# Nine opening products of zeros, 512 columns wide, become 36 of 128 columns

## The chip, the cores and the metric

The kernel runs on one core of a Trainium2 chip. The metric is the device time of one execution in microseconds, from several runs of which the median is given. Engines are named as in the profile: PE is TensorE's matmul row, PEld its weight loads, DVE is VectorE, ACT is ScalarE, POOL is GpSimd, SP is SyncE, which here issues most of the DMAs.

## The reference

For x of 2048 rows and 512 columns, the output mixes two branches with a gate per row. Branch a is a filter in the two-dimensional Fourier domain, branch b is a two-layer network with 1792 hidden features.

```python
g = sigmoid((x * gate_w).sum(-1, keepdims=True))
X = rfft2(x) * (w_r + 1j * w_i)          # 2048 x 257
a = irfft2(X, s=(2048, 512))
h = gelu(x @ w1 + b1)                    # 2048 x 1792
b = h @ w2 + b2
return g * a + (1 - g) * b
```

The opening products that this case is about compute nothing of this: both operands are zeros and the result is never read.

## The kernel before, in words

The 2048 rows are cut into 16 tiles of 128. A forward pass per tile folds x into even and odd parts on VectorE (`eo`, then `w`, L593 and L596), multiplies them by a cosine and sine table `cf` on PE (results `pd`), and transforms along the rows with a table `tf` (results `py`). Twiddles, the filter, and the inverse (`pz`, `pa`) follow later. The network's first layer is done for two of its fourteen feature blocks as plain products (results `ph`), for the others by a seven-product scheme (`nu`, `ux`); the second layer gives `po`, in the last group `dm`, `dn`, `dx`, `dz` and `dl`.

Most products are in the type float32r, which holds fewer bits than float32; a float32 operand is then split into a high and a low part and takes three products. Some, among them `pd` and the first `ph` products from the raw tile `war`, take plain float32 operands. All matmuls go through the helper `mm`, so the profile gives them one line, L420; the tile names tell them apart. A plain float32 matmul stands in the profile as two pairs of weight load and product, a float32r one as one pair.

Every piece of work is a step that is added to a graph with its engine, an estimated cost, what it reads and what it writes. The order in which the steps are emitted is a list of step numbers written out in the source (`ORDER`), and the buffers' places are another (`SLOTS`). The costs in the `add` calls are not used when the order is replayed. Each engine runs its own instructions in that order.

At the start, VectorE sets a 128 by 128 tile `zero` to 0 (L501). As soon as it is there, the step `warm` issues nine matmuls of `zero` by `zero` into a PSUM bank named `none` (`WARM = 9`). The moving operand is `zero` read four times over by an access pattern that repeats it, so that each has 512 columns. Three filler steps of 256 columns (`FILL = 3`) are in the order too: one directly behind the nine, one after the first four records of `ph`, one among the first `pd` records. On PE the order at the start is thus: nine opening products, a filler, four records of `ph`, a filler, twelve of `ph`, six of `pd`, a filler, more of `pd`.

Meanwhile the first x tile (`xf`, in two halves), two halves of the raw first-layer weights (`war`), the table `cf` and the gate weights (`g`) arrive by DMA. VectorE copies four sums of the gate weights into spare columns of `cf` (L547); the first `pd` product reads `cf` and waits for that copy. Behind it, ACT and DVE split `pd` into a high and a low part (`zb`), and PE takes those for `py`.

Of the kernel before, what the change touches and what calls it, by code (L numbers as in the profile page):

```python
# [354 lines left out]
def tile_kernel(ctx: ExitStack, tc: tile.TileContext, xt, xc, w1, w2, b1, b2, x0g, wf, wrev, out, consts):  # L355
# [18 lines left out]
    def buf(tag, shape, dt=F32, name="", parts=1, pool=None, cls=None, full=False, onto=False):  # L374
        slots.setdefault(tag, 1)
        return Buf(g, pool or (pp if tag in PSUM else sb if tag in whole else sc), tag, shape, dt, name, parts, cls, full, onto)

    def bank(shape, name, cls, full=False, onto=False, parts=1):
        return buf("ps", shape, F32, name, parts, None, cls, full, onto)
# [39 lines left out]
    def mm(ps, w, x, start, stop, **more):  # L419
        pe.matmul(ps, w, x, start=start, stop=stop, **more)  # L420
# [4 lines left out]
    def bcast(ap, *ns):  # L425
        return bass.AP(tensor=ap.tensor, offset=ap.offset, ap=[list(ap.ap[0]), *[[0, n] for n in ns], list(ap.ap[1])])
# [72 lines left out]
    FILL, WARM, NBARE = 3, 9, 1  # L499
    zero, none = buf("w", [P, P], F32R, "zero", cls="zero"), bank([P, 4, P], "none", "none", full=True)  # L500
# [3 lines left out]
    act_first.table = "gelu"  # L504

    def warm():
        for _ in range(WARM):
            mm(none.ap(), zero.ap(), bcast(zero.ap(), 4), True, True)

    add("pe", 0.09 + 0.427 * WARM, 0.1, warm, [zero], [none])  # L510

    for _ in range(FILL):
# [870 lines left out]
```

## Time and profile before

| | before |
|---|---|
| median of 3 runs | 354.13 us (353.65 to 354.32) |
| profiled execution, its own time | 353.74 us |
| its span, first to last instruction | 352.0 us |
| PE busy | 344.8 us, 1742 matmul records |
| PEld busy | 291.9 us, 1742 weight loads |
| DVE busy | 333.4 us |
| ACT busy | 301.6 us |
| opening products (128x512) | 9 records, 1.07 us to about 5.1 us |
| fillers (128x256) | 3 records, at 5.07, 5.60 and 8.55 us |
| first `pd` record | 7.86 us |

Busy times are unions of the records of an engine. Times in views of the profile are microseconds from the first instruction, unless a column says ns. PE works on products in a pipeline, so a record's length holds the way through the array as well as the columns; the distance from one start to the next tells what a product costs. A record may be shown to start while its engine still waits for the load or the product ahead. A view line of the form "start, length, engine, line, operation, out<-in, shapes, xcount" merges neighbours of one kind, and its length is then from the first start to the last end.

### The profile page before, as it was taken

Reading aid. Unit: us, or ns where it says so; the run is one execution under the profiler, and the core shown is the slowest. Engines: PE = TensorE matmul, PEld = TensorE weight load, DVE = VectorE, ACT = ScalarE, POOL = GpSimd, SP = SyncE. Lnnn points to the kernel's source line nnn. Section 1 sums busy time; section 2 is a strip of 40 time slices with the busy share of each in tenths; the row PEclk is TensorE's granted clock in tenths of the full one; section 3 lists DMA queues with packets and bytes.
Section 4 is the critical chain, followed back from the end, with each engine's and each line's share of the span. In section 5 each row is a group of like instructions: output and inputs, shape, how many; then the busy total and the mean of one; then the engine's idle time right before and its main releaser. Section 6 shows DMA issues by size and latency. Waiting matters only on the chain.

```text
span 352.0 us, 5796 instructions
## 1 busy us (share of the span) xinstructions
PE 344.8 (98%) x1742; PEld 291.9 (83%) x1742; DVE 333.4 (95%) x700; ACT 301.6 (86%) x631; POOL 56.6 (16%) x75
## 2 busy tenths in 40 slices
PE   8999999999999999999999999999999999999993
PEld 7988888888878888888888888888888889888883
DVE  5999999899999999999999999999999999999991
ACT  4999999999999665999759885599999999999622
POOL 2012002000003100121301301000120001463420
PEclk9999999999999999999999999999999999999998
DMA  7998896847879949999999845965582547898995
GB/s 227 378 283 287 242 300 179 226 110 288 212 239 240 183 164 294 298 225 266 240 245 239 174 116 119 298 228 180 173 175 66 148 135 208 156 152 189 196 205 198
DMA packets 47719, 74.63 MB, mean 212 GB/s; under 512 B 5544, under 2 KB 18344, under 8 KB 47688
## 3 DMA queue, kind: packets, MB, share of 16 engines
q1 hardware_dynamic: 37528, 58.42, 50.6%
q0 software_dynamic: 9728, 15.51, 27.3%
q10 hardware_dynamic: 432, 0.33, 0.3%
q8 instruction: 14, 0.23, 0.3%
q14 instruction: 17, 0.14, 0.1%
HBM read 52.02 MB, written 17.31 MB: 197 GB/s over the span
## 4 chain that ended last, share of the span: by engine, by line
PE 96%; DVE 1%; DMA 1%; issue 0%; ACT 0%; DVEq 0%
PE po L420 37%; PE uxB L420 11%; PE uxA L420 9%; PE nuB L420 8%; PE nuA L420 7%; PE pd L420 4%; PE pz L420 4%; PE py L420 3%; PE pa L420 3%; PE ph L420 3%; PE dx L420 3%; DMA xf<-in_x0g 1%; PE dm L420 1%; PE dn L420 1%; PE dz L420 1%; DVE eo L593 0%
## 5 line engine op out<-in xcount | busy, mean ns | idle before, releaser
L429 ACT ACTIVATE s<-po 128x512 f32<-128x512 f32 x40 | 23.1, 597 | 3.3 <-PE po L420 3.2
L968 ACT ACTIVATE po<-s 128x512 f32<-128x512 f32 x40 | 23.7, 598 | 0.3
L836 ACT ACTIVATE sw<-y,keep 64x512 f32<-64x512 f32 x32 | 22.5, 719 | 0.6
L775 DVE TENSOR_TENSOR m<-y,wf 128x514 f32<-128x514 f32 x32 | 21.3, 690 | 0.2
L420 PE MATMUL py<-zb,tf 128*128 128x258 f32 x96 | 20.2, 291 | 0.0
L420 PE MATMUL pd<-cf,w 128*128 128x129 f32 x128 | 18.5, 276 | 0.5 <-DVE cf L547 0.5
L420 PEld LDWEIGHTS pd<-cf,w 128*128 128x128 f32 x128 | 16.8, 191 | 1.8 <-DVE cf L547 0.7
L420 PE MATMUL pz<-tg,pq 128*128 128x128 f32 x128 | 18.3, 274 | 0.0
L420 PEld LDWEIGHTS py<-zb,tf 128*128 128x128 f32 x96 | 16.1, 189 | 2.5
L420 PEld LDWEIGHTS pz<-tg,pq 128*128 128x128 f32 x128 | 17.3, 190 | 1.0
L420 PE MATMUL nuB<-xB,wB0h 128*128 128x512 f32 x56 | 17.5, 393 | 0.0
L420 PE MATMUL pa<-zb,ci 128*128 128x256 f32 x96 | 17.0, 287 | 0.0
L420 PEld LDWEIGHTS pa<-zb,ci 128*128 128x128 f32 x96 | 15.1, 188 | 2.0
L978 ACT ACTIVATE s<-po,b2t 128x512 f32<-128x512 f32 x16 | 11.0, 693 | 6.8 <-PE po L420 6.6
L420 PE MATMUL nuA<-xA,wA0h 128*128 128x512 f32 x48 | 15.0, 393 | 0.0
L632 DVE TENSOR_TENSOR zb<-pd,zb 128x256 fp32r<-128x256 f32 x32 | 13.3, 420 | 0.8 <-ACT logit L631 0.8
L652 ACT ACTIVATE y<-pys 64x257 f32<-64x257 f32 x32 | 13.3, 417 | 0.6
L596 DVE TENSOR_TENSOR w<-eo 128x256 f32<-128x256 f32 x32 | 13.1, 419 | 0.1
L593 DVE TENSOR_TENSOR eo<-xf 128x256 f32<-128x256 f32 x32 | 12.7, 419 | 0.0
L840 DVE TENSOR_TENSOR pq<-y,sw 128x256 f32<-128x256 f32 x32 | 12.5, 416 | 0.2 <-ACT sw L836 0.2
L628 ACT ACTIVATE zb<-pd 128x256 fp32r<-128x256 f32 x32 | 12.1, 392 | 0.4 <-PE pd L420 0.4
L420 PEld LDWEIGHTS nuB<-xB,wB0h 128*128 128x128 f32 x56 | 10.4, 188 | 2.0
(595 smaller groups left out, 1262.6 us busy)
## 6 DMA issues: line engine op xcount, KB each, us to landing
wf<-in_wf SPq DMA_DIRECT2D x16, 257.0 KB
xf<-in_xt SPq DMA_DIRECT2D x14, 256.0 KB, 5.0
tf<-tf SPq DMA_DIRECT2D x16, 192.0 KB, 6.1
wrA<-in_w SPq DMA_DIRECT2D x12, 256.0 KB, 4.9
xbA<-in_xc SPq DMA_DIRECT2D x8, 256.0 KB, 5.7
xbB<-in_xc SPq DMA_DIRECT2D x8, 256.0 KB, 3.4
bacc<-s SPq DMA_DIRECT2D x8, 256.0 KB, 6.3
w<-bacc POOLq DMA_DIRECT2D x8, 256.0 KB, 4.4
```

The lines of the kernel that those rows point to most:

```text
L420: pe.matmul(ps, w, x, start=start, stop=stop, **more)
L429: a(lambda: act.activation(o.ap(), i.ap(), AF.Copy, scale=scale), n, [i], [o])
L593: v(lambda s=s, op=op: vec.tensor_tensor(eo.ap()[:, s], x.ap()[:, 0:2], x.ap()[:, 2:4], op=op), 256, [x], [(eo, s)])
L596: v(lambda s=s, op=op: vec.tensor_tensor(w.ap()[:, s], eo.ap()[:, :, 0], eo.ap()[:, :, 1], op=op), 256, [eo], [(w, s)])
L628: a(lambda c=c: act.activation(segs(xh, c), both(c), AF.Copy), 256, [ps[c]], [(xh, c)])
L632: v(lambda c=c: vec.tensor_tensor(segs(xl, c), both(c), segs(xh, c), op=ALU.subtract), 256, [ps[c], (xh, c)], [(xl, c)])
L652: a(lambda o=o, i=i: act.activation(Y[j].ap()[o:o + HP, 1], pys.ap()[i:i + HP, 1], AF.Copy), 257, [(pys, 1)], [(Y[j], 1 + k)], more=0.07)
L775: v(lambda mk=mk, k=k, y=y, w=w: vec.tensor_tensor(mk.ap(), y.ap(), w.ap()[:, k:k + 1, :ND].to_broadcast([P, 2, ND]), op=ALU.mult), 514, [ ...
L836: a(lambda sw=sw, y=y, o=o, i=i: act.activation(sw.ap()[o:o + HP], y.ap()[i:i + HP], AF.Copy, scale=keep.ap()[i:i + HP]), 512, [y, keep, * ...
L840: v(lambda sw=sw, pq_=pq_, y=y, k=k, op=op: vec.tensor_tensor(pq_.ap()[:, k], y.ap()[:, k], sw.ap()[:, 1 - k], op=op), 256, [y, TURNED[c], ...
L968: a(lambda ps=ps, n=n, o=o: act.activation(ps.ap(), o.ap()[:, n], AF.Copy), size, [o], [ps], more=0.04)
L978: a(lambda o=o, ps=ps, q=q: act.activation(o.ap(), ps.ap(), AF.Identity, bias=b2t.ap()[:, q:q + 1]), 600, [b2t, ps], [o])
```

## The change

The step `warm` issues 36 matmuls in place of nine. Each has the same 128 by 128 zeros as weights, and the same zeros, read once, as the moving operand, so 128 columns. They write the four quarters of the bank `none` in turn. The number of columns is the same in all, 9 x 512 = 36 x 128. The step keeps its place in the order, and the three fillers stay as they are.

```diff
     def warm():
-        for _ in range(WARM):
-            mm(none.ap(), zero.ap(), bcast(zero.ap(), 4), True, True)
+        for n in range(4 * WARM):
+            mm(none.ap()[:, n % 4], zero.ap(), zero.ap(), True, True)
 
     add("pe", 0.09 + 0.427 * WARM, 0.1, warm, [zero], [none])
```

## The prediction

> **What bounds the kernel now.** I read the page's head and its chain of waits first, to know which engine a lost microsecond must be lost on.
>
> ```profile
> span 352.0 us, 5796 instructions
> PE 344.8 (98%) x1742; PEld 291.9 (83%) x1742; DVE 333.4 (95%) x700; ACT 301.6 (86%) x631; POOL 56.6 (16%) x75
> PEclk9999999999999999999999999999999999999998
> PE 96%; DVE 1%; DMA 1%; issue 0%; ACT 0%; DVEq 0%
> ```
>
> TensorE (PE) is 96% of the chain that ended last. What is not PE lies at the two ends, so next comes the chain in order of time over the first 20 us.
>
> ```profile
> 0.75 3.18 DMA xf<-in_x0g
> ...
> 7.72 0.09 DVE cf L547
> 7.81 0.04 issue
> 7.86 0.94 PE pd L420 x6
> 8.79 0.12 PE none L420
> 8.91 1.11 PE pd L420 x10
> ```
>
> The opening products do not stand in it. The end is set by the first x tile landing (0.75 to 3.93), VectorE's work on it up to the copy into cf, and from 7.86 us on by PE. So PE has slack before 7.86 us. After it, I ask for the busy time of the long middle and for everything that PE's matmul and weight-load rows waited for.
>
> ```profile
> 8.00:346.00 338.00, 337.98 (x1714) 286.35 (x1715) 329.26 (x684) 297.37 (x622) 54.82 (x63) 1.00 0.79 213
> PE none L420 <- DVE zero L501: 1.1, 1, 1.1
> PE pd L420 <- DVE cf L547: 0.5, 1, 0.5
> PEld none L420 <- DVE zero L501: 1.1, 1, 1.1
> PEld pd L420 <- DVE cf L547: 0.7, 1, 0.7
> PEld pd L420 <- ACT y L648: 0.4, 2, 0.2
> PEld uxA L420 <- ACT uxA L429: 0.4, 1, 0.4
> PEld nuA L420 <- ACT gate L1292: 0.4, 1, 0.4
> PEld pown L420 <- DMA wf<-in_wf: 0.4, 1, 0.4
> PEld dx L420 <- DVE dz L1064: 0.2, 1, 0.2
> ```
>
> In the first line the matmul busy time is the first number after the width: 337.98 of 338.00 us. The second and third say that the matmuls waited twice in all, for the zeros and for cf. A delay that PE carries past 7.86 us meets almost nothing that could absorb it. The later weight-load waits are 1.8 us together; all but one are on ACT or DVE results that come from PE's own products and move with it. The one on a DMA (0.4 us) might give back up to 0.4.
>
> **The opening, product by product.** The timeline, asked in windows so narrow that each instruction stands alone (start, length, engine, what), printed to 0.01 us:
>
> ```profile
> 1.07 0.29 PEld L420 LDWEIGHTS none<-zero 128*128 128x128 f32 x1 [1.07 <-DVE zero L501]
> 1.23 0.34 PEld L420 LDWEIGHTS none<-zero 128*128 128x128 f32 x1
> 1.66 0.33 PEld L420 LDWEIGHTS none<-zero 128*128 128x128 f32 x1
> ...
> 1.66 0.63 PE L420 MATMUL none<-zero 128*128 128x512 f32 x1
> 4.65 0.63 PE L420 MATMUL none<-zero 128*128 128x512 f32 x1
> 5.07 0.33 PE L420 MATMUL none<-zero 128*128 128x256 f32 x1
> 5.24 0.27 PE L420 MATMUL ph<-xf,war 128*128 128x128 f32 x1
> 7.06 0.28 PE L420 MATMUL ph<-xf,war 128*128 128x128 f32 x1
> 7.86 0.38 PE L420 MATMUL pd<-cf,w 128*128 128x129 f32 x1 [0.52 <-DVE cf L547]
> ...
> 5.08 0.23 PEld L420 LDWEIGHTS ph<-xf,war 128*128 128x128 f32 x1
> 5.24 0.19 PEld L420 LDWEIGHTS ph<-xf,war 128*128 128x128 f32 x1
> ...
> 5.73 0.19 PEld L420 LDWEIGHTS ph<-xf,war 128*128 128x128 f32 x1
> 5.84 0.19 PEld L420 LDWEIGHTS ph<-xf,war 128*128 128x128 f32 x1
> ...
> 7.86 0.19 PEld L420 LDWEIGHTS pd<-cf,w 128*128 128x128 f32 x1 [0.71 <-DVE cf L547]
> 7.96 0.19 PEld L420 LDWEIGHTS pd<-cf,w 128*128 128x128 f32 x1
> ...
> 344.95 1.09 PE dl L420 x9
> 15.29 2.74 PE ph L420 x12
> 5.80 1.54 PE L420 MATMUL ph<-xf,war 128*128 128x128 f32 x12
> ```
>
> Four readings.
>
> First, order. Each product has a weight load of its own, even though the weights are the same zeros, and a load starts when the product before it starts: load at 1.66 with product at 1.66, load at 5.08 with product at 5.07, load at 5.24 with product at 5.24. It starts no earlier. So loads and products run one step apart, and the step is the longer of two things: the product's columns, or the load.
>
> Second, the clock. Products of 512 columns start at 1.66 and 4.65, seven steps of (4.65 - 1.66)/7 = 0.427 us. The same width later takes 2.74/12 = 0.228. The opening runs at half speed, although the page's clock row shows full speed throughout. A load is 0.33 us long in the opening and 0.19 after 5.24; the one at 5.08 is 0.23, between them. I put the change of speed at 5.15 us, 3.92 us after the first product got going at 1.23 (its load started at 1.07; the second load, which goes with the first product's start, at 1.23).
>
> Third, the load at full speed. Where PE had been waiting, a load is not covered by a product, and the step from it to the next load is the bare time from load to product: 7.96 - 7.86 = 0.10 and 5.84 - 5.73 = 0.11. I take 0.11. Products of 256 columns (dl, 1.09/9 = 0.12) and the fp32 pieces of ph (1.54 us for 12, of which the last takes 0.28: 1.26/11 = 0.115) just cover it. No product in this kernel is short enough to uncover it in a row; the change makes 36 that are.
>
> Fourth, the load at half speed. The bare first one is 1.23 - 1.07 = 0.16, but that record is 0.29 long where its neighbours are 0.33 and 0.34, so it may have begun 0.04 or 0.05 before its record, which gives 0.21. Twice the full-speed 0.10 to 0.11 gives 0.20 to 0.22. I take 0.21 and keep 0.16 as the lower end.
>
> **The change part by part.** It removes nine products of 512 columns and adds 36 of 128. Columns: 9 x 512 = 36 x 128, nothing there. Weight loads: 9 become 36, the 27 new ones are the cost. Outputs, semaphores and the other engines' work are untouched; 54 more PE instructions at the start are costed at nothing, covered by the 0.11 to 0.21 us that each pair occupies.
>
> - Width alone, at half speed: 0.427/4 = 0.107 a product, less than the load's 0.21. So the load sets the step.
> - Before 5.15 us: (5.15 - 1.23)/0.21 = 18.7 products. The other 17.3 at 0.11 take 1.91. The block ends, and the filler of 256 columns behind it starts, at 7.06 instead of 5.07: 1.99 us late.
> - That filler then runs at full speed: 0.12 instead of 5.24 - 5.07 = 0.17, which gives 0.05 back.
> - PE's cover: the last ph product starts at 7.06 and its columns are through some 0.11 later, at 7.17; the first pd product gets going at 7.96 with the second load. 7.96 - 7.17 = 0.79 us is free. With PE late, cf is there long before it is wanted, and the wait on it goes; nothing else is late next, since the DVE chain to cf uses no PE result.
> - Sum: 1.99 - 0.05 - 0.79 = +1.15 us at the first pd product, and past it all of it reaches the end.
>
> The profiled execution took 353.74 us (span 352.0 and 1.74 around it), 0.39 below the median of 354.13. Against itself the sum is 354.89; against the median it is 355.28. I forecast **355.3**.
>
> Bounds of the one unknown, the step: with 0.16 and half of it, 24.5 products are done by 5.15 and 11.5 x 0.08 = 0.92 follow, end 6.07, late 1.00, net +0.16 after the 0.05 and the 0.79 (0.84 together). With 0.22 and, at full speed, the 0.12 of dl, 17.8 and 18.2 x 0.12 = 2.18, end 7.33, late 2.26, net +1.42. I take the value near the upper end because the bare full-speed loads, 0.10 and 0.11, have no shortened record to explain away. A change of speed that comes 0.5 us earlier or later than 5.15 moves the changed kernel by 0.25 and leaves the kernel before alone, because the 0.79 covers it there.
>
> [...]
>
> **The rivals.**
>
> - *The loads are covered* (the other side: not slower). If a load took no longer than 0.107 at half speed, the 36 products would need 36 x 0.107 = 3.84 us, the block would end at 5.07 as before, and the time stays 354.1. For it: at 512 columns the half-speed steps show no trace of the load. Against it: the bare 0.16 at 1.07, and every load starting only with the product before. It decides at a step of 0.15, where the lateness just fills the 0.79.
> - *A shorter load*: step 0.16 then 0.08, net +0.2 to +0.3, 354.4, within what can be told from no change. [...] Against it: the two bare full-speed loads.
> - *The clock stays low longer.* The array's columns are then in use only half of the time (0.107 of 0.21), and if the speed depends on use, the change at 5.15 may come late. One more stretch of 3.92 us would put it at 9.07. All 36 then run at 0.21, end 8.79; the stretch from filler to the end of ph (7.17 - 5.07 = 2.10, less the 0.05), with 0.14 lost to the last 0.28 us of low speed, end at 10.98 against 7.96: +3.0, 357.1. For it: only that use halves. Against: the array is never idle for long. [...]
> - *Narrow products of this type run as slowly as plain fp32.* One fp32 product of 128 columns is two of ph's pieces, 2 x 0.11 = 0.22 at full speed, 0.43 at half. Then 9.2 are done by 5.15, 26.8 x 0.22 = 5.90 follow, end 11.05, net 5.98 - 0.84 = +5.14, 359.3. For it: no product of the one-pass type below 256 columns exists here. Against: at 256 columns (0.12 a product) it is still one pass, and nothing in the rows points to a step below.
> - *Faster*: PE cannot gain before 7.86 us because cf is not there earlier; only chance in the later order could do it.
>
> **How the numbers follow.** My forecast, +0.7 to +1.4 with PE's later waits passing it on: 0.54. Shorter load, +0.1 to +0.7: 0.15. Covered: 0.10. Clock late: 0.09. Slow type: 0.09. Faster: 0.03. About 0.2% (0.7 us) is what a measurement of this kernel can tell from no change. Same is covered and shorter load, plus 0.04 of the forecast for a partial give-back of the 0.4: 0.29. Slower is 0.50 + 0.09 + 0.09 = 0.68. The range goes from the covered case less the scatter of the runs, 353.9, to the late clock, 357.2; it leaves out the slow type and faster, 0.12.
>
> **What would show it.** In the profile after, the rows of none<-zero are 36 products of 128 columns; right if they start 0.21 apart, then 0.11, and the 256-column filler starts near 7.1 us. The wait of pd on cf disappears from PE's waits, the first pd product gets going near 9.1 us, and the span is about 353.2. A step of 0.107 shows the loads covered; 0.16 and 0.08 the shorter load; 0.21 throughout, and 0.33-long loads beyond 5.3 us, the late clock; 0.43 the slow type. The forecast also fails if pd is 1 us late but the end is not: then a wait further down took the delay in, and the weight-load waits listed above would have shrunk.

## The result and the profile after

The changed kernel takes 357.75 us (median of 6 runs, 356.28 to 358.81) against 354.02 (6 runs of the kernel before, 353.53 to 355.13). The ratio is 1.0109, with a 95% interval of 1.0090 to 1.0129: 3.73 us slower. The forecast was 355.3 with a range to 357.2, so the direction was right and the size and the range were wrong. The profiled execution took 356.28 us, the lowest of the six.

The page of the changed kernel, then its chain of waits in order of time (start, length, what):

```profile
span 354.5 us, 5850 instructions
PE 349.3 (99%) x1769; PEld 297.6 (84%) x1769; DVE 333.7 (94%) x700; ACT 301.5 (85%) x631; POOL 56.5 (16%) x75
PE 98%; ACT 0%; issue 0%; DVE 0%
```

```profile
1.07 8.26 PE none L420 x37
9.33 0.85 PE ph L420 x4
10.18 0.21 PE none L420
10.39 1.82 PE ph L420 x12
12.21 0.67 PE pd L420 x6
```

The first landing and the VectorE chain are gone from the chain; PE now holds it from 1.07 us on, and the opening alone is 8 us of it. `pd` follows `ph` without a pause (10.39 + 1.82 = 12.21), so the wait on `cf` is gone, as forecast. Single weight loads of the changed kernel, from its timeline in narrow windows:

```profile
8.70 0.33 PEld L420 LDWEIGHTS none<-zero 128*128 128x128 f32 x1
8.91 0.33 PEld L420 LDWEIGHTS ph<-xf,war 128*128 128x128 f32 x1
11.05 0.31 PEld L420 LDWEIGHTS ph<-xf,war 128*128 128x128 f32 x1
11.26 0.20 PEld L420 LDWEIGHTS ph<-xf,war 128*128 128x128 f32 x1
12.05 0.19 PEld L420 LDWEIGHTS pd<-cf,w 128*128 128x128 f32 x1
349.99 0.19 PEld L420 LDWEIGHTS dl<-gx,v1l 128*128 128x128 f32 x1
```

From the second load (1.23 us) to the one at 8.91 there are 36 steps: 7.68/36 = 0.213 us each, to the last one. The load is 0.33 us long all through and becomes short only behind 11.05. So the narrow products do wait for their loads, as forecast (0.107 us would be their columns' own step), but the change to full speed that the forecast put at 5.15 us came at 11.28. (The clock's own record in the trace, which no view prints, dates the change; the dates of changes below are from it, counted from the first instruction.) The row at 12.05 is the second load of `pd`, the mark used in the prediction; before, it stood at 7.96. The last row is the last weight load of the kernel, at 345.98 before:

```profile
345.98 0.19 PEld L420 LDWEIGHTS dl<-gx,v1l 128*128 128x128 f32 x1
```

PE is 4.09 us late at `pd` and 4.01 late at its last load, 338 us further on. The span is only 2.5 longer, because what follows the last load shrank from 352.0 - 345.98 = 6.0 us to 354.5 - 349.99 = 4.5. Two things were thus not foreseen: the clock, and the tail.

### The profile page after: what moved, and what is told of

It is laid out like the page before. It is cut to its first block, busy times and chain, and to the rows that moved or that the text cites. A ratio compares the mean times of both kernels' runs of the same rounds, so it can differ in the third digit from the quotient of the medians.

```text
span 354.5 us, 5850 instructions
## 1 busy us (share of the span) xinstructions
PE 349.3 (99%) x1769; PEld 297.6 (84%) x1769; DVE 333.7 (94%) x700; ACT 301.5 (85%) x631; POOL 56.5 (16%) x75
## 4 chain that ended last, share of the span: by engine, by line
PE 98%; ACT 0%; issue 0%; DVE 0%
PE po L420 37%; PE uxB L420 11%; PE uxA L420 9%; PE nuB L420 8%; PE nuA L420 7%; PE pd L420 4%; PE pz L420 4%; PE ph L420 4%; PE py L420 3%; PE pa L420 3%; PE dx L420 3%; PE none L420 2%; PE dm L420 1%; PE dn L420 1%; PE dz L420 1%; PE dl L420 0%
```

## The experiments

All change only the body of `warm`. "Use" below is the share of a half-speed step in which columns stream: 512 columns take 0.427 us at half speed, so 128 take 0.107 of a step of 0.213. Each expectation names its theory and rival.

**18 products of 256 columns.** Same columns as before, twice the loads, each load just covered.

```diff
+        for n in range(2 * WARM):
+            k = n % 2 * 2
+            mm(none.ap()[:, k:k + 2], zero.ap(), bcast(zero.ap(), 2), True, True)
```

> The opening is 18 products of 256 columns in place of nine of 512. Theory (use): a product at half speed lasts as long as the longer of its columns and the load beside it, here both 0.213 us, so the block ends at 5.07 us as before; the array's columns are in use all the time, so the change to full speed comes near 5.15 us as before, and the time is that of before, 354.0 within 0.5. Rival (loads or width): if it is the number of weight loads, or products narrower than 512 columns, that keeps the speed low, the block still ends at 5.07 but ph and pd run at half speed till about 11 us: half of (11 - 5.15), less the 0.79 of slack, gives +2.1, 356.1.

Measured: 352.49 us (7 runs) against 353.45 on the same chip, ratio 0.9970 (0.9959 to 0.9981). In its profile the block is not later than before, and the speed changes inside it:

```profile
3.79 0.26 PEld L420 LDWEIGHTS none<-zero 128*128 128x128 f32 x1
3.99 0.19 PEld L420 LDWEIGHTS none<-zero 128*128 128x128 f32 x1
4.57 0.19 PEld L420 LDWEIGHTS ph<-xf,war 128*128 128x128 f32 x1
```

The rival (more loads, or less than 512 columns, keep the speed low) falls. The change came at 3.94 us. That it is 1 us faster than before was in neither theory, and its profile does not show where the gain lies: it is that of the slowest of the seven runs (353.33), in which PE's weight loads wait 0.7 us for a transfer (`gx`) near the end, and PE's last load is at 346.09.

**18 products of 128 columns.** Half the columns of before; the loads make the block equally long.

```diff
+        for n in range(2 * WARM):
+            mm(none.ap()[:, n % 4], zero.ap(), zero.ap(), True, True)
```

> The opening is 18 products of 128 columns, half the columns of before. The block lasts 18 x 0.213 = 3.84 us and ends at 5.07 as before, so only the speed can differ. Theory (use): the columns are in use half of the time, which does not raise the speed; the change comes some 2 to 4 us after the full-width work begins at 5.07 (2.1 us after it in the changed kernel, 3.9 after the first product in the kernel before), that is at 7.2 to 9.0, and the time is half of the lateness less 0.79, +0.2 to +1.2. Rival (length alone, the late change in the changed kernel being chance): the change comes at 5.15 and the time is 354.0.

Measured: 353.81 us (12 runs, 352.68 to 356.25), ratio 1.0018 (1.0001 to 1.0035). The profile, which is that of its fastest run:

```profile
5.07 0.33 PEld L420 LDWEIGHTS ph<-xf,war 128*128 128x128 f32 x1
7.42 0.23 PEld L420 LDWEIGHTS ph<-xf,war 128*128 128x128 f32 x1
7.57 0.19 PEld L420 LDWEIGHTS ph<-xf,war 128*128 128x128 f32 x1
```

The block ends at 5.07 as expected, and the speed changes at 7.50. Against the kernel with 18 products of 256 columns, run on the same chip with as many PE instructions and a block no longer than 3.84 us, it is 353.81 - 352.49 = 1.3 us slower. Use, or the width that goes with it, is what is left between them. The date alone does not settle it, since an opening of full use changed as late as 7.29 us (18 wide products, below).

**36 products of 128 columns in bf16.** The changed kernel's count and columns, with loads of two bytes.

```diff
+        z = zero.ap().bitcast(mybir.dt.bfloat16)[:, :P]
+        for n in range(4 * WARM):
+            mm(none.ap()[:, n % 4], z, z, True, True)
```

> The opening is 36 products of 128 columns as in the changed kernel, but the zeros are read as bf16. If it is the length of a four-byte weight load that sets the step and a bf16 load is about half as long, the steps are 0.107 us, the block ends at 5.07, the columns are in use all the time, the speed changes near 5.15, and the time is that of before, 354.0 within 0.5. Rival (the narrow product itself, whatever its type): the step stays 0.213, the speed changes near 11 us, and the time is that of the changed kernel, 357.8 within 1.

Measured: 352.00 us (5 runs), ratio 0.9966 (0.9954 to 0.9978).

```profile
1.15 0.15 PEld L420 LDWEIGHTS <-zero 128*128 128x128 bf16 x1
1.26 0.15 PEld L420 LDWEIGHTS <-zero 128*128 128x128 bf16 x1
1.07 3.75 PEld L420 LDWEIGHTS <-zero 128*128 128x128 bf16 x36 [1.07 <-DVE zero L501]
6.49 0.28 PEld L420 LDWEIGHTS ph<-xf,war 128*128 128x128 f32 x1
345.72 0.19 PEld L420 LDWEIGHTS dl<-gx,v1l 128*128 128x128 f32 x1
```

The step is 0.107, the columns' own; all 36 fit into 3.75 us and cost nothing (PE's last load is at 345.72, against 345.98 before). So neither the number of products nor their 128 columns is the cause; the four bytes are. The edit changes the type of the product as well as that of its load. That it is the load rests on the bare four-byte loads, 0.10 to 0.11 us at full speed with no product beside them, and on the step of the next experiment. The speed changed only at 6.67 us here, and the slack covers it.

**36 products of 64 columns.**

```diff
+        for n in range(4 * WARM):
+            mm(none.ap()[:, n % 4, :P // 2], zero.ap(), zero.ap()[:, :P // 2], True, True)
```

> The opening is 36 products of 64 columns. If load and columns of neighbours run beside each other and the load is 0.213 us long, the step is 0.213 as with 128 columns, the block ends at 8.9 us, the speed changes later than that, and the time is near that of the changed kernel, 357 to 359. If load (0.107) and columns run one after the other, the step is 0.107 + 0.053 = 0.16, the block ends at 7.0, and the time is about 1.9 us less.

Measured: 357.73 us, one run.

```profile
8.70 0.33 PEld L420 LDWEIGHTS none<-zero 128*128 128x128 f32 x1
8.91 0.33 PEld L420 LDWEIGHTS ph<-xf,war 128*128 128x128 f32 x1
13.40 0.29 PEld L420 LDWEIGHTS pd<-cf,w 128*128 128x128 f32 x1
```

The block ends at 8.91, to the hundredth as with 128 columns, so the step is the same 0.213 us with 64 columns as with 128. Load and columns run beside each other here, and the load is 0.213 us at half speed.

**36 products of 192, 160 and 176 columns.** The step stays the load's 0.213; only the use changes, to 75%, 62% and 69%. The edit, for 192:

```diff
+        for n in range(4 * WARM):
+            k = n % 2 * 2
+            mm(none.ap()[:, k:k + 2, :96], zero.ap(), bcast(zero.ap()[:, :96], 2), True, True)
```

> The opening is 36 products of 192 columns. The load sets the step, 0.213 us at half speed, as with 64, 128 and 256 columns, so the columns are in use 0.16 of 0.213, 75%. So far the change to full speed came 2.3 to 5.5 us after products that use the columns all the time began, and never within the 3.8 to 7.7 us of products at half or a quarter. [...] Rival (narrowness itself: any product of less than 256 columns keeps the speed low): all 36 at 0.213.

> The opening is 36 products of 160 columns, in use 0.133 of 0.213, 62%. [...] Rival (only half use or less is too little): the change comes between 3.5 and 6.9 us.

> The opening is 36 products of 176 columns, in use 0.147 of 0.213, 69%. With 160 columns (62%) none of the 36 changed the speed, with 192 (75%) it changed 4.5 us in. Theory: the share needed lies between; if it is below 69%, the change comes between 3.5 and 6.9 us and the time is 353 to 355, if above, all 36 steps are 0.213 and the time is 356 to 358. Rival (narrowness, not use, and the one at 192 chance): as above, 356 to 358.

Measured: 353.86, 356.58 and 355.78 us, one run each (before on those chips: 353.52, 353.52, 353.66). With 192 columns the speed changes inside the block; from then on 16 loads take 1.94 us:

```profile
5.50 0.26 PEld L420 LDWEIGHTS none<-zero 128*128 128x128 f32 x1
5.68 0.19 PEld L420 LDWEIGHTS none<-zero 128*128 128x128 f32 x1
5.50 1.94 PEld L420 LDWEIGHTS none<-zero 128*128 128x128 f32 x16
```

With 160, and then with 176, it does not; the block runs to 8.91 and the change comes in `ph`:

```profile
8.91 0.33 PEld L420 LDWEIGHTS ph<-xf,war 128*128 128x128 f32 x1
11.69 0.29 PEld L420 LDWEIGHTS ph<-xf,war 128*128 128x128 f32 x1
...
10.41 0.27 PEld L420 LDWEIGHTS ph<-xf,war 128*128 128x128 f32 x1
```

Narrowness as such falls as a cause: 192 is below 256 too. At a use of 75% the speed rose 4.3 to 4.5 us into the block (at 5.50 to 5.68, less 1.23), at 69% and 62% not in 7.7 us. Each is a single run, and none of them shows why, or how much use it takes. At half use or less the speed did not rise in any of four blocks of 7.7 us (the changed kernel twice, the 64 columns, and the 36 behind nine wide products below).

**Nine wide products, then the 36 narrow ones; 18 wide, then 36 narrow.** The wide ones are as before, the narrow ones as in the change.

> The opening is the nine products of 512 columns of before and behind them the 36 of 128 of the changed kernel. The speed changes during or soon after the nine, so most of the 36 run at full speed and show the load there: 0.107 to 0.12 by the bare loads of the kernel before. At 0.11 the 36 take 4.0 us from 5.1 on, the first filler starts at about 9.1, and the time is 4.0 - 0.8 = 3.2 over before. If half use also takes the speed back within them, the last steps are 0.213 again.

> The opening is 18 products of 512 columns, then the 36 of 128. 18 wide ones last up to 7.7 us at half speed, longer than the 5.5 us within which every full-use stretch so far brought the change, so the narrow ones begin at full speed. Their step shows the load at full speed with 128 columns, expected 0.11 (0.1117 was measured with 192 columns). If half use also takes the speed back, some later steps are 0.213 or the stretch after them is; if it only fails to raise it, all 36 take 4.0 us.

Measured: 362.74 and 358.46 us, one run each. The first expectation missed. The nine wide products ended at 5.07 without a change of speed, it stayed low to the end of the 36 narrow ones (12.76), and it changed at 17.47:

```profile
12.76 0.33 PEld L420 LDWEIGHTS ph<-xf,war 128*128 128x128 f32 x1
17.24 0.31 PEld L420 LDWEIGHTS pd<-cf,w 128*128 128x128 f32 x1
```

So 3.84 us of full use were not enough here; in the kernel before, where `ph` follows them, the change came at 5.14 and, in its second profile, at 6.44. Why it came as late as 17.47 here is not shown. With 18 wide ones the speed was up before the narrow ones began, and stayed up:

```profile
7.21 0.23 PEld L420 LDWEIGHTS none<-zero 128*128 128x128 f32 x1
8.29 3.99 PEld L420 LDWEIGHTS none<-zero 128*128 128x128 f32 x35
```

The second row is from the second of these narrow steps to the end: 3.99 less the last load's 0.19, over 34 steps, is 0.112 us a step. That is the full-speed load with 128 columns. Half use for 4.0 us did not take the speed back.

**The kernel before and the changed kernel once more**, each for a second profile.

> The kernel before, unchanged, for a second profile. In the first, the last product's load starts at 345.98 us and the span ends 6.0 us later, where four of the other five profiles have 4.5 to 4.7 us and one 5.5; and the first x tile lands at 3.9 us, in the others at 3.4 to 3.7. If the time by which 18 products of 256 columns and 36 of bf16 beat it (1.0 and 1.5 us) lies in these two, they show again here; if they were chance, the tail is 4.5 to 4.7 and the first pd product comes at 7.6 to 7.8.

> The changed kernel, unchanged, for a second profile. [...] Rival (a fixed delay): the change comes at 11.2 again.

Measured: 353.26 and 357.16 us, one run each. In the kernel before, the first x tile landed earlier than in the first profile (VectorE begins on it at 3.63 us instead of 3.95), and the speed changed only at 6.44. The second load of `pd` came at 7.74 instead of 7.96, now behind PE's own work. The late landing of the first profile was thus chance. The long tail was not: it is 351.5 - 345.69 = 5.8 us here.

```profile
7.74 0.19 PEld L420 LDWEIGHTS pd<-cf,w 128*128 128x128 f32 x1
345.69 0.19 PEld L420 LDWEIGHTS dl<-gx,v1l 128*128 128x128 f32 x1
```

In the changed kernel the block ended at 8.91 again, and the speed changed at 13.28, two microseconds later than in the first profile:

```profile
8.91 0.33 PEld L420 LDWEIGHTS ph<-xf,war 128*128 128x128 f32 x1
13.18 0.24 PEld L420 LDWEIGHTS pd<-cf,w 128*128 128x128 f32 x1
350.92 0.19 PEld L420 LDWEIGHTS dl<-gx,v1l 128*128 128x128 f32 x1
```

A fixed delay falls. PE's last load is 4.9 us later than in the first profile of before, and the tail is 355.4 - 350.92 = 4.5 again.

**Nine wide products in bf16**, for the tail.

```diff
+        z = zero.ap().bitcast(mybir.dt.bfloat16)[:, :P]
+        for _ in range(WARM):
+            mm(none.ap(), z, bcast(z, 4), True, True)
```

> The opening is nine products of 512 columns as before, with the zeros read as bf16, so that PE has as many instructions as before. Eight profiles of other openings ended 4.4 to 5.5 us after the last product's load, the two of the kernel before 5.8 and 6.0, with one of the last store issues on SP 1.3 us long. Theory: this goes with how long PE's program is, whatever the opening holds; then the tail is 5.8 to 6.0 here too and the time that of before, 353.2 to 353.8. Rival (the float32r opening itself): the tail is 4.5 and the time that of the 36 bf16 products, 1.2 to 1.5 us below before.

Measured: 353.23 us (12 runs) against 353.66, ratio 0.9985 (0.9970 to 1.0000). Its span is 351.5 us, and its last load:

```profile
345.61 0.19 PEld L420 LDWEIGHTS dl<-gx,v1l 128*128 128x128 f32 x1
```

The tail is 5.9 us. Ordered by the number of opening products, tails in microseconds are: nine, 6.0, 5.8 and 5.9; 18, 5.5 and 4.7; 36, 4.4 to 4.7 in seven profiles; 45 and 54, 4.4 and 4.5. The pair that differs least is the bf16 one: 36 and nine products with the same columns, PE's last load at 345.72 and 345.61, spans of 350.2 and 351.5. In these profiles, what follows PE's end is shorter where PE's program has more opening products. SP's rows show a part of where the time goes. Of before (two rows) and of the changed kernel (two rows):

```profile
343.65 3.44 SPq L1081 DMA_DIRECT2D out<-t  x4
347.18 0.40 SPq L1078 DMA_DIRECT2D out<-t  x1
...
347.64 3.17 SPq L1081 DMA_DIRECT2D out<-t  x4
350.90 0.40 SPq L1078 DMA_DIRECT2D out<-t  x1
```

Counted from PE's last load, the last store is issued 1.20 us later before and 0.91 later in the changed kernel; the rest of the 1.5 us lies behind that issue. Why is not settled: the experiments show that the tail goes with the number of opening products, and so with the program's length, not how.

## Why the prediction was wrong

Its terms against the first profile of the changed kernel:

| term | predicted, us | measured, us |
|---|---|---|
| block longer, if the speed changes at 5.15 | +1.99 | +2.05 |
| speed still low from there to the block's end | 0 | +1.79 |
| from the filler to the second load of `pd` | -0.05 | +1.04 |
| PE's slack before `pd` | -0.79 | -0.79 |
| at the second load of `pd` | +1.15 | +4.09 |
| given back later | 0 | -0.08 |
| tail | 0 | -1.5 |
| end | +1.15 | +2.5 |

The first measured term takes 18.4 steps of 0.213 to 5.15 and 17.6 of 0.112 after it, end 7.12 against 5.07; the second is 8.91 - 7.12; the third is (12.05 - 8.91) - 2.10.

- *The order of load and product, and the load's price* were right: 0.213 at half speed and 0.112 at full, where 0.21 and 0.11 were taken. The bare 0.16 of the first load, kept as the lower bound, did not come again: the 36 steps from the second load on are 0.213.
- *The step that failed is the second reading*: 5.15 us was read off the kernel before and carried over to the changed one as if it were a date. The two profiles of the kernel before give 5.14 and 6.44, those of the changed kernel 11.28 and 13.28; what sets the date within a kernel is not shown. The prediction named a late change as its rival "the clock stays low longer", on the ground that use halves, but gave it 0.09 and sized it at one more stretch of 3.92 us, ending at 9.07. In neither profile of the changed kernel did the speed rise in the 7.7 us of the block; it rose only in the work of `ph` and `pd` behind it. So that rival too was too small, 357.1 for 357.75, and the range ended short of the result.
- *Covered loads, the shorter load and the slow type* are refuted by the step: 0.213, not 0.107, 0.16 or 0.43.
- *Passing on.* That nearly all of PE's lateness reaches PE's end was right: 4.09 at `pd`, 4.01 at the last load.
- *The tail* was taken as constant. It gave 1.5 us back, which made the error look smaller: by PE alone the change costs 4.0 and 4.9 us in the two profiles.
- *Scatter.* The changed kernel's six runs spread over 2.5 us. By the same reasoning as in the prediction, a later change of speed moves it by half of the delay, as nothing covers it any more: from 11.28 and 13.28 us that is an estimate of 1.0 us between its two profiles, and PE's last load is 350.92 - 349.99 = 0.93 later in the second. In the kernel before, 5.14 and 6.44 us made no difference that the slack did not take.

The 36 bf16 products gave the lowest time, 352.0 us, below both kernels. PE's last load is at 345.72 there, between the 345.98 and 345.69 of the kernel before, so nearly all of that gain lies in the tail.

## What to carry to other kernels

In these runs a four-byte weight load on PE cost as much as 256 columns: 0.213 us a step at half speed, with 64, 128, 160 and 176 columns as with 256, and 0.112 at full speed with 128 columns, where products of 256 take 0.12. Here a product narrower than that paid for its load, not for its columns, and by its columns' own 0.107 of 0.213 us at 128 columns it left the array idle for half of the time. So look whether narrow products can be merged, or use bf16 where the values allow: 36 bf16 products of 128 columns had a step of 0.107 and took 352.00 us, against 357.75. Where work is there to bring PE to full speed, check in a profile that it does: the openings whose columns stream all the time were followed by the change 2.7 to 6.1 us after the first product, that of nine wide products with narrow ones behind them only at 17.47 us. Before a date such as a change of clock is carried from one profile to another kernel, ask what sets it, and take a second profile of the same kernel.

## What the hardware showed that was not expected

- The speed of PE changed 2.7 to 6.1 us after the first product in the six profiles of openings whose columns stream all the time (at 3.92, 3.94, 5.14, 6.44, 6.67 and 7.29 us; the first product got going at 1.23 or a little before), the one left out being that where narrow products followed before it had changed. Among the openings of 36 four-byte products, the speed rose inside the block at a use of 75% of the step (between the loads at 5.50 and 5.68 us), and not in its 7.7 us at 69%, 62%, 50% and 25%. That use decides is the author's reading of these runs; what sets the date, and how much use it takes, they do not show.
- In the first profiles of the two kernels the trace's record of the clock has full speed from 5.14 us on, for 344.7 us (before), and from 11.28 on, for 341.3 us (changed), and 0.5 of it behind that.
- Behind the narrow blocks the speed rose in the records of `ph` and `pd`: in `ph` at 11.28 us in the first profile of the changed kernel, in `pd` at 13.28 in the second. These records have 128 and 129 columns, and before the change their step is 0.213 us like that of the narrow products (8.91 to 11.26 us, 11 steps). The author took them as full use; why the speed rose in them and not in the block is not shown.
- Once up, the speed outlasted 4.0 us of narrow products at half use (35 loads from 8.29 us on, 0.112 us a step).
- The clock row of the profile's page read full speed in every slice of every kernel but, in some, the last, also where 36 loads in a row ran at half. The trace's record of the clock begins only with the change, and the row counts what lies before as full speed. The length of a weight load (0.33 or 0.19 us) is the better sign.
- With 36 products in place of nine at PE's start, the 5.8 to 6.0 us from PE's last load to the end became 4.4 to 4.7.
